# Attention and a rational feed-forward layer on one core: score tiles of 128 queries of one head, compact q, P^T in seven groups, and three word operations per weight block

## The chip, the core and the metric

The kernel runs on one NeuronCore of one Trainium2 chip. The metric is the device time of one execution in microseconds (us). A core has five engines that run side by side and are tied together by semaphores: TensorE (PE in the profile; its weight loads are listed as PEld), VectorE (DVE), ScalarE (ACT), GpSimd (POOL) and SyncE (SP), which here issues the transfers. Matmuls write to PSUM, which has eight banks; a tile of 128 partitions by 512 float32 values fills one.

## The reference

q, k, v, a and b are float32, the two weight matrices float64. Attention is block-causal: a query block of 64 sees its own and all earlier key blocks. The feed-forward layer has a rational activation.

```python
B, H, S, D = 8, 8, 576, 64                    # q, k, v
scores = (q @ k.transpose(0, 1, 3, 2)) / sqrt(D)
scores = where(pos[:, None] // 64 >= pos[None, :] // 64, scores, -1e9)
p = exp(scores - max(scores)); attn = p / (sum(p) + 1e-9)
x = (attn @ v).transpose(0, 2, 1, 3).reshape(4608, 512)
h = x @ w_in                                  # 512 -> 2048
P = a[0] + a[1] * h + a[2] * h**2 + a[3] * h**3
Q = 1.0 + abs(b[0]) * abs(h) + abs(b[1]) * h**2
out = (P / (Q + 1e-6)) @ w_out                # 2048 -> 512
```

## The kernel before

Every matmul operand is split into a rounded high part and a remainder (names ending in h and l), and three matmuls replace one: high by high, high by low, low by high.

**Attention** runs over 32 pairs of heads (8 batches by 4 pairs). Of a pair, 128 rows hold two heads of 64 values. `load` brings q, k and v; `prep` transposes q and k on TensorE (L368, and L376 for the last 64 positions) and splits them (`put`: ScalarE rounds at L348, VectorE subtracts at L351). K becomes one tile of 128 rows by 576. q becomes `qbd`, nine block-diagonal tiles of 128 by 128: query block i of the first head sits in the upper left quarter, that of the second in the lower right, the rest is zero. So one matmul over 128 rows (L420) gives the scores of 64 queries of both heads, and no mask is needed: block i is multiplied with 64(i+1) key columns only.

A pair's nine query blocks are treated in five duos d of two items j: block 8 in two halves of 288 columns, and then blocks 7 and 0, 6 and 1, 5 and 2, 4 and 3. `scores` makes the item and its maximum (L421; L423 joins the halves of block 8), `expo` the exponentials with their sums on ScalarE (L434) and the division on POOL (L442, L447, with a reciprocal on VectorE, L443). `transp` turns a duo's probabilities around on TensorE (L456): 25 transposes per pair in ten groups of three or two, each rounded by ScalarE (L459) and subtracted by VectorE (L460) into `ptr`, P^T. `pv` multiplies with V (L471, L487), and the result goes through DRAM (`xscr`) to the feed-forward layer.

**The feed-forward layer** is done in two phases: 10 of 16 feature blocks with `wA` while attention runs, 6 with `wB` when it is over; the first phase leaves partial sums in DRAM (`pscr`). A unit of the first phase is 24 matmuls of 256 columns (`first`, L198) and 12 of 512 (`second`, L248). **Weights** are float64 in DRAM: `place` (L109 to L140) makes the two parts out of the two 32-bit words of each value, in 32 blocks of 128 by 512. Of each block, VectorE does five word operations (L123, L125, L128, L129, L130), ScalarE an absolute value (L120), an integer conversion (L132) and for `wA` a copy (L135), and POOL a maximum (L121) and a product (L136 or L138). 20 blocks are for `wA`, and 12 go to DRAM for `wB`.

**Order.** `attn_steps` counts items k, ten to a pair. `ALAG2`, `TLAG` and `OFFS` say how many items after its scores an item is exponentiated and transposed, and when the next pair is loaded and prepared. `WSTEPS` and `WB0` spread the weight blocks over items; from item 54 on feed-forward half units are emitted at a rate per item. This order is the input to a scheduler, which places each engine's instructions by the times that it expects. Score and P^T tiles take turns in the five PSUM banks of `ps_a`; the first four pairs may also use the feed-forward layer's three (`bank`).

Of the kernel before, what the change touches and what calls it, by code (L numbers as in the profile page):

```python
# [9 lines left out]
F32 = mybir.dt.float32  # L10
# [15 lines left out]
ALAG2 = 1  # L26
# [7 lines left out]
OFFS = (0, 3, 5)  # L34
TLAG = 8
# [16 lines left out]
QSCALE = 0.125  # L52
QC = 1.0 + 1e-6
# [5 lines left out]
def attn_ffn_kernel(  # L59
# [46 lines left out]
    def split_weights(pool, f0, nf, dt):  # L106
        wih, wil, woh, wol = weight_tiles(pool, f0, nf, dt)

        def place(dhi, dlo, src, nm):  # L109
# [6 lines left out]
            bt = ffn.tile([128, 512], F32, name=f"wb{nm}", tag="v")  # L116
            pt = ffn.tile([128, 512], F32, name=f"wp{nm}", tag="s")
            ai, bi, pi = at.bitcast(I32), bt.bitcast(I32), pt.bitcast(I32)

            nc.scalar.activation(out=at, in_=w1.bitcast(F32), func=AF.Abs)  # L120
            nc.gpsimd.tensor_scalar_max(at, at, WMIN)  # L121

            nc.vector.tensor_scalar(out=ai, in0=ai, scalar1=3, scalar2=0x3FFFF000,  # L123
                                    op0=ALU.logical_shift_left, op1=ALU.bitwise_and)
            nc.vector.scalar_tensor_tensor(out=bi, in0=w1, scalar=-0x40000000, in1=ai,  # L125
                                           op0=ALU.bitwise_and, op1=ALU.bitwise_or)

            nc.vector.tensor_scalar(out=ai, in0=bi, scalar1=-0x800000, scalar2=None, op0=ALU.bitwise_and)  # L128
            nc.vector.tensor_scalar(out=pi, in0=w0, scalar1=9, scalar2=None, op0=ALU.logical_shift_right)  # L129
            nc.vector.scalar_tensor_tensor(out=pi, in0=w1, scalar=23, in1=pi,  # L130
                                           op0=ALU.logical_shift_left, op1=ALU.bitwise_or)
            nc.scalar.activation(out=pt, in_=pt.bitcast(U32), func=AF.Copy, scale=2.0 ** -43)  # L132
            v3 = lambda x: x.rearrange("p (d f) -> p d f", d=nd)
            if dt is F32R:
                nc.scalar.copy(out=dhi, in_=v3(bt))  # L135
                nc.gpsimd.tensor_tensor(out=dlo, in0=v3(pt), in1=v3(at), op=ALU.mult)  # L136
            else:
                nc.gpsimd.tensor_tensor(out=v3(pt).bitcast(F32R), in0=v3(pt), in1=v3(at), op=ALU.mult)  # L138
                nc.sync.dma_start(out=dhi, in_=v3(bt))
                nc.sync.dma_start(out=dlo, in_=v3(pt))  # L140
# [154 lines left out]
    DUOS = [((8, 0, 288), (8, 288, 288))] + [((8 - d, 0, 64 * (9 - d)), (d - 1, 0, 64 * d)) for d in range(1, 5)]  # L295

    def blocks(d):
        i, x = DUOS[d][0][0], DUOS[d][1][0]
        rest = {0: ((8, 4), (8, 3)), 1: ((0, 0), (7, 3)), 2: ((1, 0), (6, 3))}.get(d, ((x, 0), (x, 1)))
        return ((i, 0), (i, 1), (i, 2)), rest  # L300

    def slot(i, kb):
        return (i, 7 + i, 14 + i, 17 + i, 16)[kb]

# [311 lines left out]
```

## Time and profile before

| what | value |
|---|---|
| runs | 1388.48, 1394.38, 1395.79 us; median 1394.38 |
| the profiled execution | 1391.85 us; its span, first to last instruction, 1390.1 us |
| mean granted TensorE clock | 0.948 of full speed |
| chain that ended last | PE 55%, DVE 17%, POOL 10%, ACT 8%, DMA 5%, issue 4% |
| first scores / last scores | 8.8 us / 951 us |

The chain follows the work that ended last back to the start, at each step to what released it. A group's row in the profile names line, engine, operation, output<-inputs and count; behind the bar stand the busy time in us and the mean of one in ns, and behind the next bar how long the engine had been idle just before and what ended that.

### The profile page before, as it was taken

The numbers are of one execution on the slowest core, as the hardware profiler recorded it, in microseconds if no ns is written. First come the engines' busy times: TensorE is split into PE (matmuls) and PEld (weight loads), VectorE is DVE, ScalarE is ACT, GpSimd is POOL, SyncE is SP. The second block draws the span as 40 slices with busy tenths as digits, with TensorE's granted clock in tenths as the row PEclk, the third lists the DMA queues.
The fourth block names the chain that finished last, engine by engine and source line by source line (L and its number), as shares of the span: only waits on it lengthen the run. The fifth ranks groups of instructions, "written<-read, shape, count | busy, mean of one in ns | idle before, by whom it ended". The sixth has DMA issues, their size and how long they took to land.

```text
span 1390.1 us, 22425 instructions
## 1 busy us (share of the span) xinstructions
PE 1264.8 (91%) x7352; PEld 1113.6 (80%) x7352; DVE 1083.2 (78%) x2080; ACT 912.9 (66%) x2154; POOL 959.4 (69%) x1080
## 2 busy tenths in 40 slices
PE   6766799899989898999899999999799999999997
PEld 5656688788878787888888889898689888888885
DVE  8999878788777889778887888887287776666674
ACT  6676767676666767668687777776256655565553
POOL 5998867687666777677776777776376655656654
PEclk9776899999999999999999999999899999999998
DMA  5455333345243433334323324322712243333332
GB/s 144 137 148 167 101 100 105 97 115 159 73 121 82 120 105 99 107 88 137 104 77 102 87 67 122 92 80 68 287 31 81 75 134 121 121 122 121 121 113 84
DMA packets 199507, 153.52 MB, mean 110 GB/s; under 512 B 128480, under 2 KB 167392, under 8 KB 199392
## 3 DMA queue, kind: packets, MB, share of 16 engines
q1 hardware_dynamic: 199328, 152.09, 37.6%
q8 instruction: 59, 0.97, 0.3%
q14 instruction: 56, 0.46, 0.1%
q0 software_dynamic: 64, 0.00, 0.0%
HBM read 98.57 MB, written 44.04 MB: 103 GB/s over the span
## 4 chain that ended last, share of the span: by engine, by line
PE 55%; DVE 17%; POOL 10%; ACT 8%; DMA 5%; issue 4%; SPq 1%; POOLq 0%; DVEq 0%; ACTq 0%
PE h L198 21%; PE o L248 20%; PE o L487 5%; PE s L420 4%; PE t L456 2%; DVE ptrl L460 2%; DVE nm L421 2%; POOL p L447 2%; ACT p L434 2%; POOL u L208 2%; DMA xt<-xh 2%; DVE v L222 1%; DVE u L221 1%; DVE s L223 1%; POOL v L207 1%
## 5 line engine op out<-in xcount | busy, mean ns | idle before, releaser
L198 PE MATMUL h<-x,wih 128*128 128x256 f32 (+1 forms) x1872 | 422.6, 316 | 20.2 <-DMA x<-xscr 10.3
L198 PEld LDWEIGHTS h<-x,wih 128*128 128x128 f32 x1872 | 319.1, 196 | 45.1 <-DMA x<-xscr 11.7
L198 PE MATMUL h<-x,wil 128*128 128x256 f32 (+1 forms) x936 | 293.9, 314 | 0.0
L231 POOL TENSOR_TENSOR gl<-s,gh 128x512 fp32r<-128x512 f32 x144 | 189.8, 1319 | 89.4 <-ACT gh L230 88.9
L447 POOL TENSOR_SCALAR p<-p,rc 128x576 f32<-128x576 f32 (+8 forms) x288 | 199.2, 703 | 68.6 <-DVE rc L443 57.5
L248 PE MATMUL o<-woh,gl 128*128 128x512 f32 x576 | 234.0, 406 | 10.5 <-POOL gl L231 10.0
L248 PE MATMUL o<-woh,gh 128*128 128x512 f32 x576 | 229.2, 398 | 0.0
L248 PE MATMUL o<-wol,gh 128*128 128x512 f32 x576 | 228.4, 397 | 0.0
L434 ACT ACTIVATE p<-s,nm 128x288 f32<-128x288 f32 (+4 forms) x320 | 160.4, 505 | 70.3 <-DVE nm L421 42.3
L208 POOL TENSOR_TENSOR u<-v,u 128x512 f32<-128x512 f32 x144 | 191.4, 1329 | 9.5
L198 PEld LDWEIGHTS h<-x,wil 128*128 128x128 f32 x936 | 182.5, 195 | 8.6
L207 POOL TENSOR_SCALAR v<-u,bab 128x512 f32<-128x512 f32 x144 | 122.0, 847 | 94.2 <-ACT u L205 91.8
L421 DVE TENSOR_REDUCE nm<-s 128x1 f32<-128x288 f32 (+4 forms) x320 | 142.7, 450 | 41.8 <-PE s L420 39.6
L209 DVE TENSOR_TENSOR s<-s,h 128x512 f32<-128x512 f32 x144 | 98.3, 683 | 97.7 <-ACT s L206 96.5
L460 DVE TENSOR_TENSOR ptrl<-t,ptrh 128x384 fp32r<-128x384 f32 (+1 forms) x320 | 147.2, 481 | 18.1 <-ACT ptrh L459 16.8
L459 ACT CAST ptrh<-t 128x384 fp32r<-128x384 f32 (+1 forms) x320 | 126.3, 430 | 49.6 <-PE t L456 49.1
L456 PE MATMUL t<-ident,p 128*128 128x128 f32 x800 | 134.5, 291 | 25.0 <-DVE ptrl L460 13.8
L215 ACT ACTIVATE v<-u,qcb 128x512 f32<-128x512 f32 x144 | 104.6, 726 | 74.4 <-POOL u L208 73.7
L230 ACT CAST gh<-s 128x512 fp32r<-128x512 f32 x144 | 89.4, 624 | 87.3 <-DVE s L223 85.1
L205 ACT ACTIVATE u<-h 128x512 f32<-128x512 f32 x144 | 86.2, 599 | 89.7 <-PE h L198 82.7
L248 PEld LDWEIGHTS o<-woh,gl 128*128 128x128 f32 x576 | 110.5, 192 | 33.9 <-POOL gl L231 14.3
L456 PEld LDWEIGHTS t<-ident,p 128*128 128x128 f32 x800 | 100.8, 148 | 43.3 <-issue 7.2
(94 smaller groups left out, 2688.7 us busy)
## 6 DMA issues: line engine op xcount, KB each, us to landing
x<-xscr SPq DMA_DIRECT2D x56, 256.0 KB, 3.7
xt<-xh SPq DMA_DIRECT2D x64, 144.0 KB, 2.4
xscr<-xh SPq DMA_DIRECT2D x64, 144.0 KB, 2.4
xscr<-xl SPq DMA_DIRECT2D x32, 288.0 KB, 2.3
pscr<-os SPq DMA_DIRECT2D x18, 512.0 KB, 2.8
pt<-pscr SPq DMA_DIRECT2D x18, 512.0 KB, 4.2
out_dram<-os SPq DMA_DIRECT2D x18, 512.0 KB, 3.0
qr<-in_q_dram SPq DMA_DIRECT2D x64, 128.0 KB, 2.5
```

The costliest lines, as they stand in the source:

```text
L198: nc.tensor.matmul(h[:, j, :], lhsT=w[:, dc, fs], rhs=xs[dc][:, hl, :], start=(dc == 0 and i == 0), stop=(dc == 3 and i == 2))
L207: nc.gpsimd.tensor_scalar(out=vt, in0=ut, scalar1=b1, scalar2=b0, op0=ALU.mult, op1=ALU.add)
L208: nc.gpsimd.tensor_tensor(out=ut, in0=vt, in1=ut, op=ALU.mult)
L215: nc.scalar.activation(out=vt, in_=ut, func=AF.Ln, bias=qcb)
L231: nc.gpsimd.tensor_tensor(out=gl.rearrange("p j t -> p (j t)"), in0=st, in1=gh.rearrange("p j t -> p (j t)").bitcast(F32), op=ALU.subtract)
L248: nc.tensor.matmul(self.o[m], lhsT=g[:, j, ms], rhs=w[:, f, :], start=(u == 0 and j == 0 and i == 0), stop=(u == nu - 1 and j == NBU[ph] - ...
L421: nc.vector.reduce_max(out=nm[:, j:j + 1], in_=ps[:, :w], axis=AX.X, negate=True)
L434: nc.scalar.activation(out=pts[i][:, c0:c0 + w], in_=s.pop((d, j2))[:, :w], func=AF.Exp, bias=nm[:, n:n + 1], scale=1.0, accum_out=sm[:, j ...
L447: nc.gpsimd.tensor_scalar(out=x, in0=x, scalar1=rc[:, j2:j2 + 1], scalar2=1.0, op0=ALU.mult, op1=ALU.mult)
L456: nc.tensor.transpose(ps[:, x, :], pts[i][:, 128 * kb:128 * kb + 128], ident)
L459: nc.scalar.copy(out=dh, in_=ps[:, :n])
L460: nc.vector.tensor_tensor(out=dl, in0=ps[:, :n], in1=dh.bitcast(F32), op=ALU.subtract)
```

## The change

There are four parts.

1. **Score tiles.** Instead of 64 queries of both heads, a tile has 128 queries of one head: `TILES` lists the query tiles 4, 3, 2, 0, 1 (tile 4 is block 8, 64 queries of both heads, as before over 128 rows with a block-diagonal `qtl`). For the others, the two heads' matmuls run over 64 rows each, the first head's on rows 0 to 63 and the second's on rows 64 to 127, written in turns, each head into a bank of its own; 128(i+1) key columns are multiplied, and a fourth matmul with `mrow` and `mcol` adds −2^30 in the 64 columns that the tile's first 64 queries must not see. The lags `ALAG2`, `OFFS` and `TLAG` get other values.
2. **Compact q.** q is kept as k is, 128 rows by 512, and no longer block-diagonal; only the last 64 queries still are, and from the second pair on two small transfers put them in place.
3. **P^T in seven groups.** The 25 transposes go in six groups of four and one of one; `ptr` is laid out by head, with key block kb's columns `PK` places apart.
4. **Weights.** The two words are shifted and joined into one float32 first; the high part is its rounding, the low part the difference. VectorE does a maximum (from POOL) and three word operations, ScalarE an absolute value and the rounding, POOL a subtraction.

```diff
-ALAG2 = 1
+ALAG2 = 2
-OFFS = (0, 3, 5)
-TLAG = 8
+OFFS = (0,5,7)
+TLAG = 7
+NEG = -float(2 ** 30)
+TILES = (4, 3, 2, 0, 1)
+PH, PK = 30, 7
...
             nc.scalar.activation(out=at, in_=w1.bitcast(F32), func=AF.Abs)
-            nc.gpsimd.tensor_scalar_max(at, at, WMIN)
-
-            nc.vector.tensor_scalar(out=ai, in0=ai, scalar1=3, scalar2=0x3FFFF000,
+            nc.vector.tensor_scalar_max(at, at, WMIN)
+
+            nc.vector.tensor_scalar(out=ai, in0=ai, scalar1=3, scalar2=0x3FFFFFF8,
                                     op0=ALU.logical_shift_left, op1=ALU.bitwise_and)
-            nc.vector.scalar_tensor_tensor(out=bi, in0=w1, scalar=-0x40000000, in1=ai,
+            nc.vector.scalar_tensor_tensor(out=ai, in0=w0, scalar=29, in1=ai,
+                                           op0=ALU.logical_shift_right, op1=ALU.bitwise_or)
+            nc.vector.scalar_tensor_tensor(out=ai, in0=w1, scalar=-0x40000000, in1=ai,
                                            op0=ALU.bitwise_and, op1=ALU.bitwise_or)
-            nc.vector.tensor_scalar(out=ai, in0=bi, scalar1=-0x800000, scalar2=None, op0=ALU.bitwise_and)
-            nc.vector.tensor_scalar(out=pi, in0=w0, scalar1=9, scalar2=None, op0=ALU.logical_shift_right)
-            nc.vector.scalar_tensor_tensor(out=pi, in0=w1, scalar=23, in1=pi,
-                                           op0=ALU.logical_shift_left, op1=ALU.bitwise_or)
-            nc.scalar.activation(out=pt, in_=pt.bitcast(U32), func=AF.Copy, scale=2.0 ** -43)
...
-                nc.scalar.copy(out=dhi, in_=v3(bt))
-                nc.gpsimd.tensor_tensor(out=dlo, in0=v3(pt), in1=v3(at), op=ALU.mult)
+                nc.scalar.copy(out=dhi, in_=v3(at))
+                nc.gpsimd.tensor_tensor(out=dlo, in0=v3(at), in1=dhi.bitcast(F32), op=ALU.subtract)
...
+    def groups(d):
+        i = TILES[d]
+        if i == 4:
+            return [[(4, 0, kb) for kb in range(4)], [(4, 0, 4)]]
+        if i == 3:
+            return [[(3, h, kb) for kb in range(4)] for h in range(2)]
+        g = [[(i, h, kb) for h in range(2) for kb in range(2)]] if i else []
+        if i in (0, 2) and set(TILES[:d + 1]) >= {0, 2}:
+            g.append([(x, h, x) for h in range(2) for x in (0, 2)])
+        return g
...
-            if which == 0:
-                for j in range(2):
-                    js = slice(64 * j, 64 * j + 64)
-                    put(qh[js, 0:8, js], ql[js, 0:8, js], ps[js].rearrange("p (c t) -> p c t", c=8), QSCALE)
-            else:
-                put(kh[:, 0:512], kl[:, 0:512], ps, 1.0)
+            put(x[:, 0, 0:512], x[:, 1, 0:512], ps, (QSCALE, 1.0)[which])
+            if which == 1:
...
+                if p > 0:
+                    for js in halves:
+                        nc.sync.dma_start(out=qd[js, :, js].bitcast(F32), in_=qc[js].bitcast(F32))
...
-            for n, (x, y) in enumerate(((qh, kh), (qh, kl), (ql, kh))):
-                nc.tensor.matmul(ps[:, :w], lhsT=x[:, i, :], rhs=y[:, c0:c0 + w], start=(n == 0), stop=(n == 2))
-            nc.vector.reduce_max(out=nm[:, j:j + 1], in_=ps[:, :w], axis=AX.X, negate=True)
...
+                    for n, (x, y) in enumerate(((0, 0), (0, 1), (1, 0))):
+                        for h in range(2):
+                            hs = slice(64 * h, 64 * h + 64)
+                            nc.tensor.matmul(s[d, h][:, :w], lhsT=q[hs, x, 128 * i:128 * i + 128],
+                                             rhs=k[hs, y, 0:w], start=(n == 0), stop=False)
+                    for h in range(2):
+                        hs = slice(64 * h, 64 * h + 64)
+                        nc.tensor.matmul(s[d, h][:, w - 64:w], lhsT=mrow[hs], rhs=mcol[hs], start=False, stop=True)
+            nc.vector.reduce_max(out=nm[:, j:j + 1], in_=s[d, j][:, :w], axis=AX.X, negate=True)
```

What the scheduler makes of it is shown at three places. The first two are on TensorE; in the changed kernel L444 are the score matmuls over 64 rows, L448 the mask matmuls, L498 the transposes, and s_1_0 and s_1_1 are the two heads of the second query tile. Before, the score matmuls of one pair's second half of block 8 and of block 7:

```order
L420 MATMUL s_0_1_2448<-k_2200,qbd0h 128x288 x2
L420 MATMUL s_0_1_2448<-k_2200,qbd0l 128x288
L420 MATMUL s_1_0_2501<-k_2200,qbd0h 128x512 x2
L420 MATMUL s_1_0_2501<-k_2200,qbd0l 128x512
L198 MATMUL h_1_1_3076<-x_1_0_2704,wih_148 128x256 x2
```

Now, about the same place in the program:

```order
L498 MATMUL t_2_0_2389<-ident,p_128 128x128 x4
L444 MATMUL s_1_0_2398<-k_2161,q_2160 128x512 x3
L448 MATMUL s_1_0_2398<-mcol,mrow 128x64
L444 MATMUL s_1_1_2399<-k_2161,q_2160 128x512 x3
L448 MATMUL s_1_1_2399<-mcol,mrow 128x64
L249 MATMUL o_0_0_2443<-woh_144,gl_0_4_2955 128x512
```

The kernel's text writes the heads in turns; in this tile the scheduler has put all of the first head ahead of the second. It does so in 78 of the 128 tiles of this kind, and leaves them strictly in turns in 37. One of these is the third query tile (384 columns) of a pair near the middle; before, two score tiles of such a pair:

```order
L376 MATMUL tp_2_8623<-ident,tr_8422 128x128
L420 MATMUL s_2_1_8632<-k_8153,qbd1h 128x128 x2
L420 MATMUL s_2_1_8632<-k_8153,qbd1l 128x128
L420 MATMUL s_3_0_8689<-k_8153,qbd1h 128x384 x2
L420 MATMUL s_3_0_8689<-k_8153,qbd1l 128x384
L456 MATMUL t_4_0_8694<-ident,p_132 128x128 x3
```

Now:

```order
L498 MATMUL t_3_0_8437<-ident,p_128 128x128
L444 MATMUL s_2_0_8447<-k_8077,q_8076 128x384
L444 MATMUL s_2_1_8448<-k_8077,q_8076 128x384
L444 MATMUL s_2_0_8447<-k_8077,q_8076 128x384
L444 MATMUL s_2_1_8448<-k_8077,q_8076 128x384
L444 MATMUL s_2_0_8447<-k_8077,q_8076 128x384
L444 MATMUL s_2_1_8448<-k_8077,q_8076 128x384
L448 MATMUL s_2_0_8447<-mcol,mrow 128x64
L448 MATMUL s_2_1_8448<-mcol,mrow 128x64
L199 MATMUL h_8_4_8468<-x_8_0_7710,wih_142 128x256 x2
```

Three matmuls over 128 rows have become six over 64 in turns, with two for the mask, between matmuls over 128 rows. In all, runs of 64-row matmuls begin 163 times in the order.

The third place is VectorE at the first weight block (names wai, wbi, wpi). Before, three of its five operations (L129, L130, L123; the other two come 6 and 13 rows on):

```order
L129 TENSOR_SCALAR wpi_0_0_341<-sti_0_0_337 128x512
L351 SCALAR_TENSOR_TENSOR qbd1l<-tp_0_239,qbd1h 64x8x64
L421 TENSOR_REDUCE nm_2_260<-s_2_0_262 128x1
L130 SCALAR_TENSOR_TENSOR wpi_0_0_341<-sti_0_0_337,wpi_0_0_341 128x512
L351 SCALAR_TENSOR_TENSOR k_238<-tp_1_267,k_238 128x512
L421 TENSOR_REDUCE nm_2_260<-s_2_1_283 128x1
L351 SCALAR_TENSOR_TENSOR k_238<-tp_2_274,k_238 128x64
L351 SCALAR_TENSOR_TENSOR qbd1l<-tp_2_274,qbd1h 64x64 x2
L123 TENSOR_SCALAR wai_0_0_339<-wai_0_0_339 128x512
```

Now, with the maximum of the second block (L122) among them:

```order
L124 TENSOR_SCALAR wai_0_0_339<-wai_0_0_339 128x512
L359 SCALAR_TENSOR_TENSOR k_253<-tp_1_282,k_253 128x512
L359 SCALAR_TENSOR_TENSOR k_253<-tp_2_289,k_253 128x64
L359 SCALAR_TENSOR_TENSOR qc_291<-tp_2_289,qc_291 128x64
L451 TENSOR_TENSOR nm_0_204<-nm_0_204 128x1
L126 SCALAR_TENSOR_TENSOR wai_0_0_339<-sti_0_0_337,wai_0_0_339 128x512
L122 TENSOR_SCALAR wai_0_2_577<-wai_0_2_577 128x512
L128 SCALAR_TENSOR_TENSOR wai_0_0_339<-sti_0_0_337,wai_0_0_339 128x512
```

The block's operations follow each other on one tile instead of three, and of q only the 64-column tail (qc) is split beside k here; its 512 columns are one operation at another place instead of two.

More of the change, by code (lines that the diff above doesn't have):

```diff
@@ new lines, in place @@
+                nc.gpsimd.tensor_tensor(out=dlo, in0=v3(at), in1=dhi.bitcast(F32), op=ALU.subtract)
+            else:
+                bt = ffn.tile([128, 512], F32R, name=f"wb{nm}", tag="v")
+                pt = ffn.tile([128, 512], F32R, name=f"wp{nm}", tag="s")
+                nc.scalar.copy(out=bt, in_=at)
+                nc.gpsimd.tensor_tensor(out=pt, in0=at, in1=bt.bitcast(F32), op=ALU.subtract)
+                nc.sync.dma_start(out=dhi, in_=v3(bt).bitcast(F32))
+                nc.sync.dma_start(out=dlo, in_=v3(pt).bitcast(F32))
@@ L361, in prep @@
             if which == 0:
-                s["k"] = att.tile([128, 2, S], F32R, name=f"k{p}", tag="k", bufs=2)
-            kh, kl = s["k"][:, 0], s["k"][:, 1]
-            qh, ql = qbd[p % 2]
+                s["q"], s["k"] = (att.tile([128, 2, n], F32R, name=f"{x}{p}", tag=x, bufs=2)
+                                  for x, n in (("q", 512), ("k", S)))
+            x = s["qk"[which]]
             raw = (s["qr"], s["kr"])[which]
@@ L428, in expo @@
             nm, sm = s[d]
-            if d == 0 and j == 0:
+            i = TILES[d]
+            if i == 4 and j == 0:
                 return
-            for j2 in (0, 1) if d == 0 else (j,):
-                i, c0, w = DUOS[d][j2]
-                n = 0 if d == 0 else j2
-                nc.scalar.activation(out=pts[i][:, c0:c0 + w], in_=s.pop((d, j2))[:, :w], func=AF.Exp,
+            for j2 in (0, 1) if i == 4 else (j,):
+                n, w = (0, 288) if i == 4 else (j2, 128 * (i + 1))
+                dst = pts[4][:, 288 * j2:288 * j2 + 288] if i == 4 else pts[i][:, j2]
+                nc.scalar.activation(out=dst, in_=s.pop((d, j2))[:, :w], func=AF.Exp,
                                      bias=nm[:, n:n + 1], scale=1.0, accum_out=sm[:, j2:j2 + 1])
@@ L450, in transp @@
         def transp(p, d):
             st_[p].pop(d)
-            for gi, g in enumerate(blocks(d)):
+            for gi, g in enumerate(groups(d)):
                 n = len(g)
-                ps = bank(p, f"t{p}_{d}_{gi}").rearrange("p (c t) -> p c t", c=4)
-                for x, (i, kb) in enumerate(g):
-                    nc.tensor.transpose(ps[:, x, :], pts[i][:, 128 * kb:128 * kb + 128], ident)
-                s0, s1 = slot(*g[0]), slot(*g[1])
-                dh, dl = (x[:, s0:s0 + (n - 1) * (s1 - s0) + 1:s1 - s0, :] for x in ptr)
-                nc.scalar.copy(out=dh, in_=ps[:, :n])
-                nc.vector.tensor_tensor(out=dl, in0=ps[:, :n], in1=dh.bitcast(F32), op=ALU.subtract)
+                ps = bank(p, f"t{p}_{d}_{gi}")
+                for x, (i, h, kb) in enumerate(g):
+                    src = pts[4] if i == 4 else pts[i][:, h]
+                    nc.tensor.transpose(ps[:, 128 * x:128 * x + 128], src[:, 128 * kb:128 * kb + 128], ident)
+                dh, dl = (spot(x, g) for x in ptr)
+                sh = {(4, 4): "p (k h t) -> p k h t", (4, 1): "p (h t) -> p h t", (3, 4): "p (k t) -> p k t"}
+                kw = dict(h=2, t=64) if g[0][0] == 4 and n == 4 else dict(h=2) if g[0][0] == 4 else \
+                    dict(k=4) if g[0][0] == 3 else dict(h=2, k=2)
+                src = ps[:, :128 * n].rearrange(sh.get((g[0][0], n), "p (h k t) -> p h k t"), **kw)
+                nc.scalar.copy(out=dh, in_=src)
+                nc.vector.tensor_tensor(out=dl, in0=src, in1=dh.bitcast(F32), op=ALU.subtract)
```

106 lines of the change are left out of this document (63 added, 43 removed).

## Prediction

> **What bounds the kernel now.** I read the stages first, then what sets the pace in each. The page gives the busy time of each engine; its boundaries in time come from the trace's table of windows (busy time per engine in each window, then the granted TensorE clock).
>
> ```profile
> PE 1264.8 (91%) x7352; PEld 1113.6 (80%) x7352; DVE 1083.2 (78%) x2080; ACT 912.9 (66%) x2154; POOL 959.4 (69%) x1080
> ```
> ```profile
> 54.00:162.00 108.00, 77.68 (x398) 67.37 (x397) 104.97 (x223) 76.76 (x211) 94.70 (x103) 0.76 0.53 150
> 162.00:660.00 498.00, 452.73 (x2863) 406.61 (x2864) 402.05 (x836) 345.95 (x897) 353.89 (x435) 0.95 0.39 106
> 660.00:970.00 310.00, 301.17 (x2014) 274.17 (x2014) 251.56 (x526) 228.44 (x583) 224.63 (x278) 0.99 0.32 88
> 970.00:1390.00 420.00, 398.64 (x1919) 336.25 (x1918) 278.25 (x392) 225.00 (x364) 249.36 (x215) 0.98 0.35 118
> ```
>
> Up to 162 us there is almost only attention and weight conversion. VectorE is busy 104.97 of 108 us there, TensorE 78: VectorE sets the pace. From 162 to 970 us feed-forward units fill the gaps of attention, and TensorE is busy 91%, later 97%; it is near its limit, with VectorE at 81%. After 970 us only feed-forward work is left, which the change does not touch. So a saving on VectorE pays fully before 162 us and partly until 970, and work added to TensorE is paid for after 162 us.
>
> How much of a saving on the other engines becomes time between 162 and 970 us can be read from the kernel itself, because the conversions end there. The windows count one line's instructions (VectorE busy, count behind x, granted clock): first L423, which runs once per pair of heads, then L125, once in each of 32 conversions.
>
> ```profile
> 255.00:661.00 406.00, 8.00 (x13) 0.95 0.39 108
> 661.00:929.00 268.00, 3.24 (x9) 0.99 0.34 91
> ```
> ```profile
> 0.00:162.00 162.00, 18.43 (x19) 0.79 0.53 146
> 255.00:661.00 406.00, 6.89 (x9) 0.95 0.39 108
> 661.00:929.00 268.00, 0.68 (x1) 0.99 0.34 91
> ```
>
> A pair takes 406/13 = 31.2 us in the first stretch and 268/9 = 29.8 in the second; 9/13 − 1/9 = 0.58 more conversions per pair go with those 1.4 us, so one conversion costs 2.5 us of time. The groups by shape (busy us, mean ns after the bar) give what a conversion and a pair take on VectorE, and the POOL operation that the change moves:
>
> ```profile
> L460 DVE TENSOR_TENSOR ptrl<-t,ptrh 128x384 fp32r<-128x384 f32 x160 | 87.9, 549 | 16.6 <-ACT ptrh L459 15.5
> L460 DVE TENSOR_TENSOR ptrl<-t,ptrh 128x256 fp32r<-128x256 f32 x160 | 65.9, 412 | 1.5 <-ACT ptrh L459 1.3
> ...
> L351 DVE SCALAR_TENSOR_TENSOR qbd0l<-tp,qbd0h 64x512 fp32r<-64x512 f32 x32 | 21.9, 685 | 1.3 <-ACT qbd0h L348 0.7
> L351 DVE SCALAR_TENSOR_TENSOR k<-tp,k 128x512 fp32r<-128x512 f32 x32 | 21.8, 682 | 2.5 <-ACT k L348 2.3
> L421 DVE TENSOR_REDUCE nm<-s 128x1 f32<-128x512 f32 x32 | 21.8, 680 | 1.3 <-PE s L420 1.2
> ...
> L123 DVE TENSOR_SCALAR wai<-wai 128x512 int32<-128x512 int32 x16 | 16.4, 1027 | 3.2 <-POOL wai L121 2.8
> L125 DVE SCALAR_TENSOR_TENSOR wbo<-sto,wao 128x512 int32<-128x512 int32 x16 | 15.2, 951 | 0.1
> L130 DVE SCALAR_TENSOR_TENSOR wpi<-sti,wpi 128x512 int32<-128x512 int32 x16 | 14.1, 882 | 0.0
> ...
> L421 DVE TENSOR_REDUCE nm<-s 128x1 f32<-128x128 f32 x32 | 9.0, 282 | 5.0 <-PE s L420 4.8
> L128 DVE TENSOR_SCALAR wao<-wbo 128x512 int32<-128x512 int32 x16 | 9.0, 562 | 0.1
> L128 DVE TENSOR_SCALAR wai<-wbi 128x512 int32<-128x512 int32 x16 | 8.9, 558 | 0.1
> L129 DVE TENSOR_SCALAR wpi<-sti 128x512 int32<-128x512 int32 x16 | 8.0, 501 | 0.7 <-DMA sti<-in_moe_w_in_dram 0.5
> ...
> L351 DVE SCALAR_TENSOR_TENSOR qbd0l<-tp,qbd0h 64x64 fp32r<-64x64 f32 x32 | 6.9, 217 | 0.2
> ```
> ```profile
> L121 POOL TENSOR_SCALAR wai<-wai 128x512 f32<-128x512 f32 x16 | 24.8, 1551 | 3.5 <-ACT wai L120 3.5
> ```
>
> The five operations of a conversion are L123, L125, L130, L128 and L129: 1.03 + 0.95 + 0.88 + 0.56 + 0.50 = 3.92 us of VectorE. So 2.5/3.92 = 0.64 us of time come with each us of VectorE work, POOL and ScalarE scaling along. I use 0.64 as the rate of exchange between 162 and 970 us.
>
> **Conversions.** Two scalar operations (L128, L129) and one two-tensor operation (L130) go; a maximum comes over from POOL and a two-tensor shift-or is added. The trace has no maximum on VectorE: the shortest one-tensor row here is 0.50 us, the longest 1.03. I take 0.56, that of L128, which has one operation too; the ends move a conversion by −0.06 and +0.47 us. Then the maximum stands for L128, the added shift-or for L130, and L129 is what is saved: 0.50 us of VectorE per conversion. POOL loses 1.55 us. On ScalarE a rounding copy takes the place of an integer conversion or stays; I cost that at nothing, since ScalarE is the least busy engine beside them before 162 us (76.76 of 108).
>
> **Scores and P^T on VectorE, per pair.** P^T: 128 columns cost 0.549 − 0.412 = 0.137 us, so a group of 512 takes 0.686 and one of 128 takes 0.275. Before: 5 x (0.549 + 0.412) = 4.81 us; after: 6 x 0.686 + 0.275 = 4.39, that is −0.41. Compact q: before 2 x 0.685 + 2 x 0.217 = 1.80, after 0.682 + 0.217 = 0.90 (64 rows cost what 128 do), that is −0.91. Maxima: the ten tiles are 2880 columns wide before and 3136 after, and a column costs (680 − 282)/384 = 1.04 ns, so +0.27. Together −1.05 us per pair. ScalarE does the same three steps, and its rows change alike; POOL scales 256 columns more. Neither is the busiest engine in any stage, so both stand in the rate of exchange and not in a term of their own.
>
> The compact tail of q reaches its place by two more transfers per pair on SP's queue, behind a wait for VectorE's remainder; behind them stand transfers of xt and V. The prep that issues them comes three steps (of ten to a pair) ahead of the scores that read them, so I cost them at nothing. Without that cover a transfer of this size costs its landing, 2.3 us, once per pair.
>
> ```profile
> tr<-in_q_dram SPq DMA_DIRECT2D x32, 32.0 KB, 2.3
> ```
>
> **TensorE.** The start times in the trace's timeline give the slot that each matmul takes at full clock (start us, duration us; x2 means two in a row).
>
> ```profile
> 600.53 0.40 PE L198 MATMUL h<-x,wih 128*128 128x256 f32 x2
> 600.76 0.28 PE L198 MATMUL h<-x,wil 128*128 128x256 f32 x1
> ...
> 603.14 0.39 PE L420 MATMUL s<-k,qbd0l 128*128 128x512 f32 x1
> 603.37 0.28 PE L198 MATMUL h<-x,wih 128*128 128x256 f32 x1
> ...
> 608.94 0.39 PE L420 MATMUL s<-k,qbd0h 128*128 128x64 f32 x2
> 609.17 0.28 PE L420 MATMUL s<-k,qbd0l 128*128 128x64 f32 x1
> ```
>
> Slots: 256 columns (600.76 − 600.53)/2 = 0.115 us, 512 columns 603.37 − 603.14 = 0.23, 64 columns (609.17 − 608.94)/2 = 0.115. So there is a floor of 0.115, and above 256 columns each costs 0.45 ns: 0.129 for 288, 0.144 for 320, 0.172 for 384, 0.201 for 448. Before, a pair's thirty score matmuls take 3 x (2 x 0.129 + 0.23 + 0.201 + 0.172 + 0.144 + 0.115 + 3 x 0.115) = 4.40 us. After, one after the other: 6 x 0.129 + 6 x (0.23 + 0.172 + 0.115 + 0.115) + 8 mask matmuls x 0.115 = 5.49, that is **+1.09**. That they run over 64 rows pays only where the two heads alternate and the chip runs them beside each other, which no row here shows. The built order lets them alternate strictly in 37 of the 128 tiles (2 of width 512, 15 of 384, 14 of 256, 6 of 128) and puts one head wholly behind the other in 78. If alternating heads overlap with the floor kept for each load of weights, only the wide ones gain: 2 x 0.69 + 15 x 0.34 = 6.5 us in all, 0.20 per pair, which leaves +0.89. If they overlap wholly, the 37 give 2 x 0.81 + 15 x 0.63 + 14 x 0.46 + 6 x 0.46 = 20 us, and in the other 91 the first head's mask can run beside the second head, 0.115 x 91 = 10 us: 0.95 per pair, which leaves +0.15. The bounds are +0.15 and +1.09; as no row has a load of 64 rows, I take the middle, **+0.6**.
>
> The Trainium skill, page "TensorE: Matmul & The Clock Gate", section "LDWEIGHTS (loading the stationary operand)", says that the load's time goes by its columns and not by its rows. The trace agrees in kind: 0.115 us for 64 columns as for 256, where that page would have 0.107 for 128 columns of weights (an estimate from its formula). By it the floor stays and the charge is +0.89, 7 us more in the sum below.
>
> **The sum.** Before 162 us: 6 pairs x 1.05 + 19 conversions x 0.50 = 15.8 us less VectorE, at 97% busy −15. From 162 to 970 us: 26 pairs x 1.05 + 13 x 0.50 = 33.8 us, at 0.64 −22. TensorE +0.6 x 26 = +15.6, times its busy share of 0.93: +14. Together −23 us. The profiled execution took 1391.85 us (span 1390.1), so **1369 us**; the runs' median, 1394.38, lies 2.5 us above that execution. Where the built order leaves three more feed-forward units behind attention, that is work moved, not added.
>
> **Rivals.**
> *Both reliefs pay in full.* Heads overlap wholly and, TensorE having room again, VectorE's relief counts at 1: −15 − 34 + 0.15 x 26 = −45, so 1347 us. For it: 45 us of idle TensorE between 162 and 660 us (498 − 452.73). Against it: the 78 tiles.
>
> *The change doesn't do what it says.* "In turns" holds for 37 tiles of 128; if nothing overlaps, TensorE is charged +1.09 x 26 x 0.93 = +26: 1381 us. With VectorE's relief at half the rate as well, −15 − 11 + 26 = 0: 1392.
>
> *Changing between 128 and 64 rows costs a gap.* The order changes into 64-row matmuls 163 times and out of them as often. If each change waits for the array to empty, its price is bounded by the part of a matmul that the next one now hides: 0.28 us of duration less 0.115 of slot is 0.16 (the row at 600.76). About 270 of the 326 changes lie behind 162 us: 270 x 0.16 = +43, so 1412 us, **slower**. It cancels the forecast's gain from 23/270 = 0.085 us for each change. No row of before has 64-row matmuls, so none speaks for or against it.
>
> The Trainium skill, page "TensorEngine Tiling (Array Packing)", section "Key Properties", says that changing the tiling mode drains TensorE, without a price; it speaks for this rival, and no run here shows it yet.
>
> A smaller one: score tiles take two of five banks at once and hold them one step longer, so that transposes wait for the exponential to free a bank.
>
> ```profile
> PE tp L368 <- ACT p L434: 6.0, 7, 1.7
> ```
>
> These waits (total us, times, longest), 6 us between 162 and 970 us, would have to grow to five times that to undo the forecast.
>
> **How the numbers follow.** Forecast, 1357 to 1384 us: 0.42. Both in full, 1335 to 1357: 0.20. Nothing overlaps, 1378 to 1396: 0.18. Changes cost a gap, 1392 to 1420: 0.15. Banks or a cause not named: 0.05. A measurement here tells about 0.5% from no change: faster means under 1387, slower over 1401. From the cases: faster 0.42 + 0.20 + 0.06 (a third of that case) = 0.68, same 0.18, slower 0.14. The range leaves out the lower third of the second case and the upper part of the gap's: 1343 to 1406.
>
> **What would show it.** VectorE busy in all should fall by about 32 x 1.55 = 50 us, and the seventh pair, whose minimum follows at 162 us now, should come about 15 us earlier. If heads overlap, a strictly alternating 384-column tile takes clearly under 6 x 0.172 us for its six matmuls; if changes cost a gap, the first full-height matmul behind a 64-row group starts clearly over 0.115 us behind the mask. The forecast is wrong if pairs take over 31 us between 255 and 661 us with VectorE less busy than before.

## The result, and the profile after

| | us |
|---|---|
| before, timed beside it | median 1391.43 (1386.4 to 1395.79) |
| changed kernel | median 1353.67 (1350.24 to 1356.66, 4 runs) |
| ratio | 0.9729, 95% interval 0.9681 to 0.9777 |
| profiled execution of the changed kernel | 1356.66, span 1354.9, mean granted clock 0.961 |

One run of the kernel before, beside e5 to e8, took 2015.0 us at a granted clock of 0.555 and is left out of every comparison. The kernel is faster by 2.7%, about 38 us. The time lies in the predicted range, 15 us under the forecast. The page of the changed kernel gives the busy time of each engine, and behind it stand the same windows as in the prediction (busy time per engine, then granted clock).

```profile
PE 1276.6 (94%) x7608; PEld 1101.5 (81%) x7608; DVE 1027.8 (76%) x1879; ACT 874.6 (65%) x1975; POOL 891.8 (66%) x1056
```
```profile
54.00:162.00 108.00, 89.01 (x469) 75.08 (x468) 95.30 (x200) 70.24 (x190) 73.40 (x98) 0.75 0.57 156
162.00:660.00 498.00, 477.79 (x3203) 417.67 (x3202) 408.41 (x798) 354.53 (x879) 357.88 (x455) 0.98 0.42 116
660.00:970.00 310.00, 299.02 (x1969) 265.21 (x1968) 214.74 (x418) 203.75 (x471) 194.72 (x246) 0.97 0.38 109
970.00:1350.00 380.00, 373.42 (x1783) 314.17 (x1781) 268.84 (x377) 213.64 (x347) 233.10 (x204) 1.00 0.31 103
```

VectorE lost 1083.2 − 1027.8 = 55 us of work, POOL 68, ScalarE 38. Before 162 us VectorE is busy 95.30 of 108 us, no longer 104.97, and TensorE 89.01 instead of 77.68. From 162 to 660 us TensorE's idle time fell from 45 us to 20, and its granted clock rose from 0.95 to 0.98.

The joining of the halves of block 8 (L423 before, L451 now) runs once per pair. Here are its runs up to 170 us in both kernels (durations; first and last start):

```profile
L423 DVE TENSOR_TENSOR nm<-nm x7: 144/159/2337, 12.0 to 162.2; 128x1 f32<-128x1 f32 x7
```
```profile
L451 DVE TENSOR_TENSOR nm<-nm x7: 137/153/390, 19.2 to 152.9; 128x1 f32<-128x1 f32 x7
```

The seventh pair comes at 152.9 us instead of 162.2, 9.3 us earlier. Counted in the traces, 48 feed-forward matmuls have run by then in both, so this is gain and not work put off. The 32nd pair comes at 886 us instead of 931. Of these 45 us, 15 are feed-forward work put off: 2364 of its matmuls have run by then, 2463 before, and a unit of 36 takes 24 x 0.115 + 12 x 0.23 = 5.5 us. So 30 us are gained by the 32nd pair: 9 before 162 us, 21 between. The last 5 of the 35 between the two profiled executions come behind it, where the change touches nothing and the granted clock went from 0.98 to 1.00.

The pace in the middle, counted by the same line:

```profile
230.00:614.00 384.00, 6.22 (x13) 0.98 0.42 117
614.00:885.00 271.00, 2.86 (x9) 0.97 0.35 93
```

A pair takes 384/13 = 29.5 us now (31.2 before) and 271/9 = 30.1 later (29.8 before). By the prediction's way of reading, a conversion costs nothing in pace any more; what that reading left out is said below.

### The profile page after: what moved, and what is told of

Its sections match the earlier page's. It is cut to its first block, busy times and chain, and to the rows that moved or that the text cites. A ratio compares the mean times of both kernels' runs of the same rounds, so it can differ in the third digit from the quotient of the medians.

```text
span 1354.9 us, 22624 instructions
## 1 busy us (share of the span) xinstructions
PE 1276.6 (94%) x7608; PEld 1101.5 (81%) x7608; DVE 1027.8 (76%) x1879; ACT 874.6 (65%) x1975; POOL 891.8 (66%) x1056
## 4 chain that ended last, share of the span: by engine, by line
PE 63%; DVE 14%; POOL 8%; ACT 6%; DMA 4%; issue 4%; SPq 1%; POOLq 0%; DVEq 0%; ACTq 0%
PE h L199 24%; PE o L249 22%; PE o L532 5%; PE s L444 5%; PE t L498 3%; DVE nm L449 2%; DVE ptrl L505 2%; POOL gl L232 2%; PE tp L376 2%; POOL u L209 2%; POOL p L474 1%; ACT p L462 1%; DVE v L223 1%; DVE s L224 1%; POOL xl L539 1%
## 5 line engine op out<-in xcount | busy, mean ns | idle before, releaser
L199 PE MATMUL h<-x,wih 128*128 128x256 f32 (+1 forms) x1872 | 417.5, 315 | 12.4 <-DVE s L211 10.4
L199 PEld LDWEIGHTS h<-x,wih 128*128 128x128 f32 x1872 | 314.1, 194 | 38.7 <-issue 12.0
L474 POOL TENSOR_SCALAR p<-p,rc 128x128 f32<-128x128 f32 (+4 forms) x288 | 193.7, 684 | 69.2 <-DVE rc L471 52.0
L462 ACT ACTIVATE p<-s,nm 128x288 f32<-128x288 f32 (+4 forms) x320 | 167.0, 529 | 55.0 <-DVE nm L449 42.8
L449 DVE TENSOR_REDUCE nm<-s 128x1 f32<-128x288 f32 (+4 forms) x320 | 146.5, 476 | 43.8 <-PE s L448 34.3
L208 POOL TENSOR_SCALAR v<-u,bab 128x512 f32<-128x512 f32 x144 | 114.3, 794 | 92.8 <-ACT u L206 89.6
L444 PE MATMUL s<-k,q 64*128 64x512 f32 (+3 forms) x768 | 138.7, 371 | 12.5 <-ACT p L462 9.6
L505 DVE TENSOR_TENSOR ptrl<-t,ptrh 128x512 fp32r<-128x512 f32 (+1 forms) x224 | 138.0, 625 | 10.6 <-ACT ptrh L504 9.6
L498 PE MATMUL t<-ident,p 128*128 128x128 f32 x800 | 128.8, 287 | 16.8 <-DVE ptrl L505 7.7
L504 ACT CAST ptrh<-t 128x512 fp32r<-128x512 f32 (+1 forms) x224 | 116.7, 544 | 20.3 <-PE t L498 19.6
```

Of the source, the lines that this page charges most:

```text
L199: nc.tensor.matmul(h[:, j, :], lhsT=w[:, dc, fs], rhs=xs[dc][:, hl, :], start=(dc == 0 and i == 0), stop=(dc == 3 and i == 2))
L208: nc.gpsimd.tensor_scalar(out=vt, in0=ut, scalar1=b1, scalar2=b0, op0=ALU.mult, op1=ALU.add)
L444: nc.tensor.matmul(s[d, h][:, :w], lhsT=q[hs, x, 128 * i:128 * i + 128], rhs=k[hs, y, 0:w], start=(n == 0), stop=False)
L449: nc.vector.reduce_max(out=nm[:, j:j + 1], in_=s[d, j][:, :w], axis=AX.X, negate=True)
L462: nc.scalar.activation(out=dst, in_=s.pop((d, j2))[:, :w], func=AF.Exp, bias=nm[:, n:n + 1], scale=1.0, accum_out=sm[:, j2:j2 + 1])
L474: nc.gpsimd.tensor_scalar(out=x, in0=x, scalar1=rc[:, j2:j2 + 1], scalar2=1.0, op0=ALU.mult, op1=ALU.mult)
```

## The experiments

Times are compared with the runs of the kernel before on the same chip; "−38" means 38 us less than its median there. The ratios stand as recorded, with their 95% intervals, and can differ from the medians' difference by a few us (e1's 0.9706 would be −41).

### The parts apart

**e1** is the kernel before with the new conversion of the weights alone; **e2** is the changed kernel with the old conversion, so with the changes to scores, q, P^T and lags alone.

```diff
 e1, against before
-            nc.gpsimd.tensor_scalar_max(at, at, WMIN)
+            nc.vector.tensor_scalar_max(at, at, WMIN)
...
+            nc.vector.scalar_tensor_tensor(out=ai, in0=w0, scalar=29, in1=ai, ...)
+            nc.vector.scalar_tensor_tensor(out=ai, in0=w1, scalar=-0x40000000, in1=ai, ...)
...
+                nc.gpsimd.tensor_tensor(out=dlo, in0=v3(at), in1=dhi.bitcast(F32), op=ALU.subtract)
 e2, against the changed kernel: the same lines the other way round
```

> The kernel before with the changed weight conversion alone (three word operations and the maximum on VectorE, no maximum on POOL, one conversion less on ScalarE). By the prediction's sum, which counts VectorE alone: 19 x 0.50 us before 162 us and 13 x 0.50 x 0.64 behind, 14 us faster, about 1377 us; VectorE busy 16 us less. Rival, that POOL's 1.55 us and the shorter chain of a block count as well: 25 us faster, about 1366 us, with pairs closer together only where conversions run, up to 600 us. Rival, that conversions hide behind attention: within 5 us of before.

> The changed kernel with the conversion of before, so score tiles, compact q, seven groups and the lags alone. If the parts add up and the conversion is worth what VectorE loses (14 us): about 1368 us. If the conversion is worth 25 us: about 1379 us. If the score part carries all of the gain: about 1354 us.

e1 took 1352.98 us, −38 (ratio 0.9706, 0.9661 to 0.9751); e2 1381.82, −9 (0.9931, 0.9904 to 0.9957). **The conversion alone brings as much as the whole change**, and the other three parts, worth 9 us by themselves, add nothing beside it. Page and middle window of e1:

```profile
PE 1253.2 (93%) x7352; PEld 1101.2 (81%) x7352; DVE 1062.3 (79%) x2048; ACT 903.3 (67%) x2134; POOL 899.6 (67%) x1048
```
```profile
162.00:660.00 498.00, 464.37 (x2989) 415.92 (x2988) 406.55 (x850) 355.48 (x919) 346.85 (x435) 0.97 0.39 108
```

VectorE lost only 21 us of work, 0.65 us per block; 38 us of time is more than that relief gives even at a rate of 1. POOL lost 60 us, and the granted clock from 162 to 660 us is 0.97, where it was 0.95.

### The conversion taken apart

**e5** moves only the maximum from POOL to VectorE; **e6** makes only the three word operations and leaves the maximum on POOL; **e7** is e1 with POOL kept as busy as before by three small maxima per block which nobody waits for (extra work, no result).

```diff
 e5, against before; e1 is e6 with the same line changed
-            nc.gpsimd.tensor_scalar_max(at, at, WMIN)
+            nc.vector.tensor_scalar_max(at, at, WMIN)
 e7, against e1
+            for _ in range(3):
+                nc.gpsimd.tensor_scalar_max(spare, w1[:, 0:64].bitcast(F32), WMIN)
```

> The kernel before with one edit: the maximum of a weight block on VectorE instead of POOL (POOL 1.55 us less per block, VectorE some 0.8 us more, the five word operations as before). Theory, that POOL's time and the shorter way of a block count and VectorE's does not decide: most of the 38 us that the conversion gave, about 1363 us. Rival, that VectorE's work decides: VectorE is busy 97% before 162 us, and 0.8 us more per block costs it 15 us there, so about 1400 us.

> The kernel before with the three word operations, but the maximum still on POOL: VectorE loses two one-tensor operations per block (1.06 us), ScalarE as in the change, POOL keeps its 1.55 us. Theory, that POOL counts: about 1380 us (VectorE's and ScalarE's share alone). Rival, that VectorE's work decides: as good as the change's conversion or better, 1350 us or less, since VectorE has 0.56 to 0.9 us less to do than there.

> The changed conversion in the kernel before, and on POOL three maxima of 64 columns per block that nobody waits for (about 1.5 us per block, as much as the maximum took that is now on VectorE). If POOL's busy time is what the conversion set free: back by 1.5 us x 32 x 0.64 = 30 us, about 1383 us. If it is the way of a block from engine to engine (one step less through POOL): within 7 us of 1353 us.

e5 took 1384.22 us, −8 (0.9947, 0.9928 to 0.9966); e6 1384.26, −8 (0.9951, 0.9931 to 0.9972); e7 1360.43, −32 (0.9773, 0.9745 to 0.9801). The pages of the three and the middle windows of e5 and e6:

```profile
PE 1257.3 (91%) x7352; PEld 1104.7 (80%) x7352; DVE 1095.8 (79%) x2112; ACT 916.7 (66%) x2154; POOL 911.2 (66%) x1048
```
```profile
PE 1269.4 (92%) x7352; PEld 1114.5 (80%) x7352; DVE 1059.9 (76%) x2016; ACT 905.2 (65%) x2134; POOL 947.8 (68%) x1080
```
```profile
PE 1260.9 (93%) x7352; PEld 1106.5 (81%) x7352; DVE 1060.5 (78%) x2048; ACT 904.2 (67%) x2134; POOL 937.9 (69%) x1145
```
```profile
162.00:660.00 498.00, 455.46 (x2920) 407.09 (x2919) 414.02 (x861) 352.81 (x911) 346.58 (x429) 0.96 0.39 108
```
```profile
162.00:660.00 498.00, 452.31 (x2829) 405.12 (x2829) 388.89 (x805) 345.80 (x892) 353.78 (x432) 0.93 0.39 107
```

Three things follow. In e5 VectorE is 13 us *busier* than before and the kernel does not get slower, it even gains 8. In e6 VectorE has 23 us less work than before, and only 8 us of time come of it. The two halves together give 38, not 17. And e7 has 38 us of POOL's work back and loses 6 us of e1's 38: POOL's being busy is not the larger part.

Where the time goes is seen by stage, in one profiled execution each (e6's is the slowest of its seven runs). The gains are against the kernel before (162.2 us with 48 feed-forward matmuls done, and 930.8 with 2463); each of these matmuls done more or less is counted at 5.5/36 us.

| | 7th pair, us (matmuls) | 32nd pair, us (matmuls) | gained by the 7th | from 7th to 32nd | behind it |
|---|---|---|---|---|---|
| e5, maximum moved | 171.9 (84) | 927.3 (2496) | −4 | +13 | −1 |
| e6, words alone | 145.8 (24) | 924.1 (2394) | +13 | −17 | +7 |
| e1, both | 147.0 (43) | 889.9 (2394) | +14 | +16 | +8 |
| changed kernel | 152.9 (48) | 885.8 (2364) | +9 | +21 | +5 |

Up to the seventh pair, where VectorE bounds, the halves behave as the prediction thought: less work on VectorE pays, and more work costs a little. What it didn't foresee happens behind, where TensorE bounds. There the granted clock takes part. In these traces and that of the kernel before, the clock records show TensorE's clock granted either in full or by half, and behind 162 us every stretch at half clock follows 3.4 us in which TensorE was busy 60% or less: such a wait can be paid for a second time. There are 14 such stretches in the kernel before (without the end of the run), 11 in e5, 15 in e6, 8 in e1 and 6 in the changed kernel. From 162 to 970 us the clock withholds 29 us of TensorE's full speed before, 21 in e5, 38 in e6, 19 in e1 and in the changed kernel. Since TensorE is busy over 90% there, about half of each entry under "from 7th to 32nd" can be this (an estimate: 8, −9, 10 and 10 us).

So the gain of e1 is partly fewer waits and partly the clock that fewer waits keep up. Which waits they are the runs don't show. That the steps of a block stand in a chain over three engines, and only a chain shortened everywhere pays, is argued and not tested by itself. A rival is not tested either: 20 of the 32 blocks now need one working tile instead of three, and these tiles share their buffers, two of each kind, with the feed-forward units; e6 has that too and gains 8. e6 gives one hint against any simple answer: its 21st pair comes at 575 us and not at 605, with 93 fewer feed-forward matmuls done, so about 16 us are gained by then (30.6 less 93/36 x 5.5); more than that is lost again up to the 32nd pair, where few conversions are left. That made the order itself a suspect.

### The order alone

Each edit makes the scheduler sort the whole program anew. **n1 to n4** are the kernel before, e1, e6 and the changed kernel with two numbers of the input order changed; instructions and amount of work are the same.

```diff
-W0 = 36
+W0 = 34
-WB0 = 80
+WB0 = 82
```

> The kernel before with two numbers of the order changed: the weight blocks of the first layer start two items earlier (W0 34 for 36) and those of the second two items later (WB0 82 for 80). Instructions and work are the same; only the order in which they stand on the engines is sorted anew. Theory A (a part of each step measured so far is the new order and not the work): the time moves by up to 10 to 20 us in either direction from 1392. Theory B (the differences are the work's own): 1385 to 1399.

> The new weight conversion alone (e1, 1353.0) with the same two numbers changed. Theory A: anywhere between 1340 and 1370, and the 38 us that the conversion gave are then partly the order's. Theory B: 1346 to 1360.

> The three word operations alone with the maximum still on POOL (e6, 1384.3) with the same two numbers changed. Theory A: the loss after pair 20, a stretch with hardly any conversions, goes away, and the time comes to about 1365. Theory B (words and maximum only pay together): 1377 to 1391.

> The changed kernel (1353.7) with the same two numbers changed. Theory A: 1340 to 1370, and the comparison of the changed kernel with the conversion alone (0.7 us apart) is then no finer than that. Theory B: 1347 to 1361.

| kernel | as it was, to before | shifted, to before | ratio shifted |
|---|---|---|---|
| before (n1) | 0 | +5.0 | 1.0035 (1.0011 to 1.0058) |
| new conversion alone (n2) | −38.1 | −36.9 | 0.9739 (0.9699 to 0.9779) |
| words alone (n3) | −8.4 | −13.1 | 0.9908 (0.9879 to 0.9937) |
| changed kernel (n4) | −37.8 | −29.4 | 0.9796 (0.9761 to 0.9832) |

A new order with the same work moves the time by −5 to +8 us. That is less than theory A's 10 to 20 us and more than the differences of some experiments. It is one shift of four kernels, so the range is a lower bound. It limits what the others can say: the gain of the conversion (38 and 37) is its own; most of the excess over its halves probably is too (38 against 17, or 37 against 21 with n3's 13), though e5 was not shifted; e7's 6 us are within an order's luck, and the 8 or 9 us of e5, e6 and e2 hardly beyond it. The score, q and P^T part brings nothing that shows beside the new conversion: 0 us without the shift, 8 us slower with it (n4 against n2).

### Scores over 64 rows

The prediction thought that the two heads overlap only where they stand strictly in turns in the order. **e3** forces that in all tiles, **e4** forces the opposite, all four matmuls of the first head ahead of the second's. `behind` ties an instruction to its forerunner in the order.

```diff
-                    for n, (x, y) in enumerate(((0, 0), (0, 1), (1, 0))):
-                        for h in range(2):
 e3
+                    for n, h in [(n, h) for n in range(4) for h in range(2)]:
 e4
+                    for n, h in [(n, h) for h in range(2) for n in range(4)]:
...
+                        if last is not None:
+                            behind(mm, last)
+                        last = mm
```

> The changed kernel with the eight matmuls of each 128-query tile held strictly in turns (first head, second head, and so on) in all 128 tiles, not only in the 37 that the scheduler left so. In the changed kernel's trace matmuls of two heads in turns start 3 ns apart, so each tile should cost TensorE half its serial slots: score matmuls 32 x about 3.1 us instead of 32 x 4.2. If TensorE bounds the attention: some 25 us faster than the changed kernel, about 1328 us. If TensorE's time is given back as waits (two heads' maxima fall due at once on VectorE, two banks are freed late): within 7 us of it.

> The changed kernel with all four matmuls of the first head held ahead of the second head's in every tile, so that next to nothing overlaps (a mask beside the second head's first matmul). If overlap is what keeps the price of the new tiles low: score matmuls cost TensorE 1.1 us more per pair, 25 us slower, about 1379 us. If overlap decides nothing (TensorE's slots are not what bounds): within 7 us of the changed kernel.

e4 took 1352.85 us, the same as the changed kernel; e3 1364.26, 11 us slower (0.9798, 0.975 to 0.9846, against 0.9729), little beyond an order's luck and far from the 25 us that it was to gain. The timeline of TensorE shows why the order of the heads does not matter where they stand side by side (start us, duration us, operation, columns, count). First a tile of the changed kernel that the scheduler has mixed (first head, first, second, second, first, second):

```profile
525.19 0.80 PE L444 MATMUL s<-k,q 64*128 64x384 f32 x6
525.82 0.20 PE L448 MATMUL s<-mcol,mrow 64*128 64x64 f32 x2
525.95 0.50 PE L249 MATMUL o<-woh,gh 128*128 128x512 f32 x1
```

And one of e4, whose built order is this:

```
L446 MATMUL s_2_0_6834<-k_6466,q_6465 128x384 x3
L449 MATMUL s_2_0_6834<-mcol,mrow 128x64
L446 MATMUL s_2_1_6835<-k_6466,q_6465 128x384 x3
L449 MATMUL s_2_1_6835<-mcol,mrow 128x64
L249 MATMUL o_6_0_6925<-woh_144,gh_6_1_6861 128x512
```
```profile
529.78 0.60 PE L503 MATMUL t<-ident,p 128*128 128x128 f32 x4
530.31 0.81 PE L446 MATMUL s<-k,q 64*128 64x384 f32 x6
530.95 0.21 PE L449 MATMUL s<-mcol,mrow 64*128 64x64 f32 x2
531.08 0.50 PE L249 MATMUL o<-woh,gh 128*128 128x512 f32 x1
```

In both, six matmuls of 384 columns take 0.63 to 0.64 us up to the mask, where six one after the other would take 6 x 0.172 = 1.03. In e4 the first head's mask, which stands ahead of the whole second head in the order, runs only when all six are under way; the records start the first matmuls of the two heads 13 ns apart. The records do not name the head; that one of each head runs is read from the starts in twos and from the masks, of which none runs as the fourth. So the chip lets the second head pass, as far as the records tell.

It does so only where no other matmul stands between the heads. Of the changed kernel's 78 tiles with one head behind the other, 41 are unbroken in the built order, and 77 of their 123 pairs of score matmuls start within 40 ns of each other; in the 37 where the scheduler has put other matmuls between, none do. In the 35 tiles unbroken and in turns all 105 do. In e4 95 tiles are unbroken, with 241 of 285 pairs.

Why e3 does not gain although its score matmuls' slots add up to 116 us and e4's to about 134 is seen at its other end. Forced turns are cut in pieces in the built order, probably because the second head's bank is expected to be free later:

```profile
318.60 0.49 PE L446 MATMUL s<-k,q 64*128 64x512 f32 x1
319.02 0.50 PE L199 MATMUL h<-x,wih 128*128 128x256 f32 x2
...
320.88 0.96 PE L446 MATMUL s<-k,q 64*128 64x512 f32 x5
321.45 0.42 PE L449 MATMUL s<-mcol,mrow 64*128 64x64 f32 x2
```

A lone 512-column score matmul goes ahead here, and the next full-height one starts 0.42 us behind it, where a slot of that width is 0.23. In e3 53 runs of 64-row matmuls end so, behind a wide matmul and not behind a mask; in e4 one does. Over their slots, entries and exits take 40 us in e3 and 27 in e4, by the starts in the trace each counted at 0.3 us at most. So 13 of e3's 18 us of shorter slots are given back there; why it ends 11 us slower is not settled.

### What the relief of VectorE is worth

**e8** is the changed kernel with the work of q's split and of three P^T groups per pair put back in twice as many instructions: the same data, five more operations per pair on VectorE and five on ScalarE.

```diff
-            put(x[:, 0, 0:512], x[:, 1, 0:512], ps, (QSCALE, 1.0)[which])
+            for js in (slice(0, 64), slice(64, 128)) if which == 0 else (slice(0, 128),):
+                put(x[js, 0, 0:512], x[js, 1, 0:512], ps[js], (QSCALE, 1.0)[which])
...
-                nc.scalar.copy(out=dh, in_=src)
-                nc.vector.tensor_tensor(out=dl, in0=src, in1=dh.bitcast(F32), op=ALU.subtract)
+                cuts = [(0, 2), (2, 4)] if g[0][0] >= 3 and n == 4 else [None]
```

> The changed kernel with its row tiles and layout, but q's high and low parts and the tail again in two operations of 64 rows each, and three of the seven P^T groups copied in two halves (ten operations of ScalarE and of VectorE, the transposes' banks as they are): VectorE has 1.3 us more per pair, ScalarE as much. If that relief is worth its time at the prediction's rate of 0.64: 26 us slower, about 1380 us. If beside the new conversion neither VectorE nor ScalarE bounds: within 7 us of 1354 us.

```profile
PE 1280.2 (93%) x7608; PEld 1100.0 (80%) x7608; DVE 1061.3 (77%) x2038; ACT 913.5 (67%) x2134; POOL 886.3 (65%) x1056
```

VectorE has 1061.3 − 1027.8 = 33.5 us more work (the prediction's 32 x 1.05), and the time is 1376.11, −17 (0.9895, 0.9854 to 0.9936): 21 us of the gain are gone, 0.63 us for each us of VectorE (0.69 by the ratios). The granted clock is no rival here, 0.960 in both kernels' medians, but ScalarE has 39 us more work too, and an order's luck of 5 to 8 us is in the difference. So the relief is there, with about the worth that it was given. Since the whole score part adds nothing that shows beside the new conversion, its 64-row tiles, masks and lags should take about as much back; that is inferred from e8 and e1, not measured in one run. The lags were not tried by themselves.

## Why the prediction was right, and where it was off

**The bound and the stages** held. Relief on VectorE paid before 162 us (e6, e1) and partly behind (e8). Behind the attention, where the change touches nothing, the profiled execution still gained 5 us, with a higher granted clock.

**Durations taken from rows of other shapes** held. These are the groups after (busy us, mean ns):

```profile
L505 DVE TENSOR_TENSOR ptrl<-t,ptrh 128x512 fp32r<-128x512 f32 x192 | 130.4, 683 | 10.6 <-ACT ptrh L504 9.6
L359 DVE SCALAR_TENSOR_TENSOR q<-tp,q 128x512 fp32r<-128x512 f32 x32 | 21.8, 681 | 1.8 <-ACT q L356 1.7
...
L122 DVE TENSOR_SCALAR wao<-wao 128x512 f32<-128x512 f32 x16 | 14.7, 921 | 0.0
L126 DVE SCALAR_TENSOR_TENSOR wai<-sti,wai 128x512 int32<-128x512 int32 x16 | 14.2, 885 | 0.2
L122 DVE TENSOR_SCALAR wai<-wai 128x512 f32<-128x512 f32 x16 | 12.7, 792 | 6.9 <-ACT wai L121 6.8
```

A P^T group of 512 columns takes 0.683 us (0.686 was worked out), q's split 0.681 (0.682). The maximum takes 0.79 to 0.92 us and not 0.56, inside its bounds. VectorE lost 55 us, where 50 were expected.

**Scores, q and P^T** were the sum −6 (six pairs before 162 us) −17 (26 x 1.05 x 0.64) +14 (TensorE) = −9; alone, they measured −9 (e2), a match within an order's luck.

**The rate of 0.64** came out well, but by luck. It put the whole difference in pace, 31.2 against 29.8 us per pair, on the conversions. The traces of before hold two more terms. From 255 to 661 us there are 1204 feed-forward matmuls, 93 for each of 13 pairs; from 661 to 929 us 940, 104 for each of 9: 12 more per pair, 1.8 us that hide a part of the conversions' price. And the clock of 0.95 withholds 22 us in the first stretch, 1.7 per pair, and 1.7 us in the second, 0.2 per pair: 1.5 us that count as their price. The two nearly cancel. e8 is compatible with the rate: six pairs at 0.97 and 26 at 0.64 would make 24 us of its 33.5, and 21 came.

**TensorE's charge** was mis-sized inside that sum. It was +0.6 us per pair. The slots of the score matmuls add up to about 143 us before and 135 after at full clock (a slot counted at no more than 1.1 times the prediction's), −0.2 per pair and below the lower bound of +0.15. Whole overlap would have made some 100 us (half of 5.49 − 0.77 per pair, plus 0.77); 223 of 384 pairs of score matmuls start together, not only in tiles in turns, but also head after head where no other matmul stands between. The rival "it does not do what it says" fell with that, as it took all 78 tiles head after head for serial. The Trainium skill, page "TensorE: Matmul & The Clock Gate", section "LDWEIGHTS (loading the stationary operand)", says that a load's time goes by its columns, and the prediction made of it a floor for each load and +0.89. That floor is not what the trace shows: in turns, the six 256-column matmuls at 601.22 us below take 0.46 us up to the mask and not 6 x 0.115 = 0.69, so two loads over different rows share one floor. Of a single load the trace says nothing against the section.

**The gap at a change of height** is real, on the way in. Some starts of the changed kernel:

```profile
600.52 0.76 PE L498 MATMUL t<-ident,p 128*128 128x128 f32 x5
601.22 0.62 PE L444 MATMUL s<-k,q 64*128 64x256 f32 x6
601.68 0.19 PE L448 MATMUL s<-mcol,mrow 64*128 64x64 f32 x2
601.80 0.50 PE L249 MATMUL o<-woh,gl 128*128 128x512 f32 x1
...
616.19 0.60 PE L498 MATMUL t<-ident,p 128*128 128x128 f32 x4
616.72 0.62 PE L444 MATMUL s<-k,q 64*128 64x384 f32 x3
```

The fourth transpose at 616.19 starts 3 x 0.11 later, at 616.52, and the score matmul 0.20 behind it. Over the trace at full clock the median from start to start is 203 ns from a 128-column matmul into 64 rows and 109 into another over 128 rows; behind 256 columns 209 and 120, behind 512 319 and 227. So an entry costs 0.09 us, and 163 entries 15 us. The way out costs next to nothing behind a mask (121 ns, against 109 to 120 without a change), which the last matmul of nearly every tile is. The rival had 0.16 for each of some 270 changes and decided from 0.085 for each; in and out together it is 0.05. The rule of the Trainium skill, page "TensorEngine Tiling (Array Packing)", section "Key Properties", that a change of mode drains the array, agrees with this trace in kind, and the price was small enough. Slots and entries together are −8 + 15 = +7 us over the 32 pairs, where +0.6 each made 19.

**The step that failed in size is the conversions' term**: 19 x 0.50 at 97% and 13 x 0.50 x 0.64 make −13 us, and e1 measured −38. It counted VectorE alone, gave POOL's 1.55 us no term, and took the clock as it was. e5, where VectorE gets busier and the kernel not slower, speaks for a price of POOL's step of its own, and e5, e6 and e1 together for prices that don't add; what carries the rest, beside the clock, stays open. Against this error of −25 us the score part's −9 went missing, and so the sum, −23, was off by only 15. That the time fell near the forecast is partly luck: one term was a third of what it measured, and another added nothing.

**By stage**: before 162 us −15 was expected and 9 came, as VectorE's idle time there grew from 3 us to 13: the relief passed the bound on to others. From 162 to 970 us −8 was expected, and 21 came, of which up to 10 are the clock's (29 us withheld before, 19 now).

**Both reliefs in full**, 1347 us, came nearest in time, and for a reason it did not name: the heads do overlap more than the forecast had, but the score part in full is not what paid.

## What to carry to other kernels

When an operation chain crosses three engines, do not price an edit by the busiest engine alone: here an edit that took 21 us of work off VectorE gave 38 us of time, and its two halves gave 8 each. Ask first which engine bounds in which stage: the operation moved onto VectorE cost some 4 us where VectorE bounds, and none showed behind. Read the granted clock beside every pace: here each fall to half came behind a stretch in which TensorE waited, so that a wait could be paid for twice. Before giving a difference of some microseconds to an edit in a kernel that a scheduler sorts, shift the order with the same work once: here that alone moved the time by −5 to +8 us. Two matmuls over different halves of the rows overlapped in turns, and mostly also head after head, but not where other matmuls stood between; so keep the two heads side by side, spend the care on how often TensorE goes into that mode, 0.09 us each time, and end each run of them with a narrow matmul.

## What the runs showed of the hardware

- Matmuls over different row halves start out of program order: in e4 13 ns apart, with three of the first head's still ahead of the second's; in the 95 unbroken tiles of e4 241 of 285 pairs start together. The Trainium skill, page "TensorE: Matmul & The Clock Gate", Part 3 "Packing small matmuls — row/col tiling", says that matmuls keep program order in their starts and ends; this trace differs.
- A change from 128 to 64 rows costs 0.09 us; the way back costs nothing measurable behind 64 columns, but the next start is 0.31 us behind a 256-column and 0.43 behind a 512-column matmul (medians of 20 and 15 in e3), against slots of 0.12 and 0.23.
- TensorE's clock is granted in full or by half. Behind 162 us of five traces (before, e1, e5, e6, changed kernel), each of the 54 stretches at half clock ahead of the run's end follows 3.4 us in which TensorE was busy at most 60%.
